# Order of all work as one table, and the units left over from both quads in one buffer

## The chip, the cores and the metric

The kernel runs on one core of a Trainium2 chip. The metric is the device time of one execution in microseconds; a median of several runs is given. TensorE (PE, with its weight loads as PEld), VectorE (DVE), ScalarE (ACT), GpSimd (POOL) and SyncE (SP, which here issues all DMAs) have a queue of instructions each and work it off in order.

## The reference, cut to what matters

Linear attention with exponential features, for 8 batches, 8 heads, 576 positions, heads of 64 and 128 features, and then a gated feed-forward layer with a convolution of width 3 along the positions:

```python
def phi(x):                                   # x: q or k
    proj = einsum('bhsd,df->bhsf', x, w_phi)
    proj = proj - max(abs(proj), axis=-1, keepdims=True)
    return concatenate([exp(proj), exp(-proj)], axis=-1)
kv  = einsum('bhsf,bhsd->bhfd', phi(k), v)
num = einsum('bhsf,bhfd->bhsd', phi(q), kv)
den = einsum('bhsf,bhf->bhs', phi(q), sum(phi(k), axis=2)) + 1e-06
x   = num / den                               # heads side by side: 512 columns
h   = maximum(x @ w_in, 0.0)                  # 512 -> 1024
c   = conv_w[0] * h[t-1] + conv_w[1] * h[t] + conv_w[2] * h[t+1]
out = (h * sigmoid(c)) @ w_out                # 1024 -> 512
```

The weights of the second part come as 64-bit floats, whose words the kernel turns into 32-bit values itself; its products run in three passes of split (high and low) values.

## The kernel before, in words

The heads of a batch form two quads of four, a quad is two head pairs. A unit is a piece of a quad's positions: units 1 and 2 hold 256 positions each, unit 0 holds the 64 positions that are left over, from both quads together. So a batch has five units of k and five of q, written (quad, unit).

A unit begins in `project`: two DMAs into the buffers "raw" (RAW of them), projections in 64\*64 tiles of TensorE into one PSUM bank for each head of a pair (the code's index i, then j), then for each of the two banks a maximum of absolute values on VectorE (L485) and a subtraction on VectorE (L492). In the first batch's k units a bank can be "biased" (KBU, 'b'): then there is no subtraction, ACT negates the maximum (L488) and takes exponentials of 128 columns straight from the bank, with the maximum as bias (L522).

`k_unit` loads v (two DMAs; V buffers), takes the exponentials (L518 or L522) and accumulates kv in 128\*64 tiles (L534 for unit 0, L549 else). After unit 2 ACT copies kv out (L557). `q_unit` transposes the features (L578, 128\*128 tiles), takes their exponentials (L582), multiplies by kv (L593, 128\*64 tiles), and divides: the denominator on ACT (L601) for the batches in DNA, on VectorE otherwise (L604), a reciprocal (L606) and a scaling into x (L607). In unit 0 each of the two banks has 256 columns, and each has its own transposes, exponentials, products and division.

Positions of all batches are then cut into 11 chunks of 320 to 448 (EDGES). `x_part` transposes x (L645) and splits it, `h_part` multiplies by w_in in eight groups h of 12 matmuls (L675), takes the positive part (L685), convolves (L688 on ACT, L698 on VectorE), takes the sigmoid and the gate (L704 to L719); `o_part` multiplies by w_out in four groups o of 24 matmuls (L739), copies out on ACT (L744) and stores. Weights are loaded and converted in `load_weight` during the first batches, mostly on VectorE and POOL with two works on ACT for each (L391, L400).

PSUM has four banks "g", two banks "m" (for h and o; x_part, the transposes and the numerators of q may use g and m, the first batch's k projections too) and two for kv.

What sets the order: the functions don't issue instructions, they add work items to a `Plan`, numbered in the order in which they are added, with a rank, a cost in nanoseconds, and the buffers that they read, write or take. `Plan.order` then plays the items through on a model of the five engines: at each step it takes the engine whose next item could begin first, and among the items that could begin then the one of the lowest rank. The table NUDGE shifts the rank of every group of items, and SLACK adds to the time at which an item of another engine releases one of TensorE. `place` picks the buffer that comes free first. The items are emitted in the order found, so each engine's queue has a fixed order in the compiled program.

Of the kernel before, what the change touches and what calls it, by code (L numbers as in the profile page):

```python
# [7 lines left out]
F32 = mybir.dt.float32  # L8
# [27 lines left out]
LANDING = 1600  # L36
PSUM_G = 4
# [12 lines left out]
SLACK = 60.0  # L50
# [9 lines left out]
RAW = 5  # L60
QS = 2
QE = 3
V = 2
OS = 2
KVF = 6
KBU = ('bb', 'bb', 'bb', 'bb', 'bb')
DNA = (0, 1)
# [3 lines left out]
NUDGE = """  # L71
# [43 lines left out]
"""  # L115
EDGE = [64 * n for n in EDGES]
# [27 lines left out]
class Plan:  # L144
# [7 lines left out]
    def add(self, eng, cost, hold, emit, reads=(), writes=(), rank=0.0, takes=(), tiled=0, table=None, after=(),  # L152
# [5 lines left out]
        w.ready = 0.0  # L158
# [75 lines left out]

    def order(self):
        engines = ("SP", "PE", "DVE", "ACT", "POOL")
# [4 lines left out]
        shift = [0.25 * int(x) for x in NUDGE.split()]  # L241
        if len(shift) == len(self.groups):
            for w in self.works:
                w.rank += shift[w.group]
# [5 lines left out]
        while len(out) < count:  # L250
# [50 lines left out]
            for o in w.before:  # L301
                o.ready = max(o.ready, w.end + HANDOVER[e, o.eng] + (SLACK if o.eng == "PE" and e != "PE" else 0))
                o.left -= 1
                if o.left == 0:
                    open_[o.eng].append(o)
# [4 lines left out]
def kernel(  # L310
# [33 lines left out]
    def dma(outp, inp, kb, rank, reads=(), writes=(), takes=()):  # L344
        cost = {130: 650, 128: 550, 64: 300, 512: 1600}.get(kb, 100 + 2 * kb)
        plan.add("SP", cost, 450, lambda: nc.sync.dma_start(out=outp(), in_=inp()), reads, writes, rank, takes)
# [108 lines left out]
    def project(src, b, qd, h, kind, r):  # L455
# [5 lines left out]
        for u in range(2):  # L461
            q, c0 = (u, 512) if h == 0 else (qd, u * 640 + (h - 1) * 256)
            dma(lambda u=u: raw[u](), lambda q=q, c0=c0: src[b, q, :, c0 : c0 + w], w // 2, r - 3.0, writes=w_(raw[u]))
        ps = [psum([P, 2 * n * F], f"p{nm}_{i}", M + G if b == 0 and kind == "k" else G) for i in range(2)]
        m = [piece([P, 2, 2 * n], F32, f"m{nm}_{i}", "m", 6) for i in range(2)]
        pr = [None if biased[i] else piece([P, 2 * n, F], F32, f"s{nm}_{i}", kind + "s", KS if kind == "k" else QS)
              for i in range(2)]

# [9 lines left out]
        for u in range(2):  # L478
            mm(222 * n, lambda u=u: emit(u), w_(raw[u], wbd_f), [(ps[0], u), (ps[1], u)], r + 0.01 * u,
               takes=[x for x in (*m, *pr) if x is not None], tiled=2)  # L480
        for i, p in enumerate(ps):
# [5 lines left out]
            if biased[i]:  # L487
                act(207, 95, lambda i=i: nc.scalar.activation(out=m[i]()[:, 1], in_=m[i]()[:, 0], func=AF.Copy, scale=-1.0),  # L488
                    [(m[i], 0)], [(m[i], 1)], ri)
            else:  # L490
                vec(*((681, 597) if n == 2 else (417, 331)),
                    lambda i=i, view=view: nc.vector.tensor_tensor(  # L492
                        out=pr[i](), in0=view(), in1=m[i]()[:, 0].unsqueeze(2).broadcast_to([P, 2 * n, F]),
                        op=ALU.subtract), w_(p) + [(m[i], 0)], w_(pr[i]), ri - 0.1)
# [4 lines left out]
    def k_unit(b, qd, h, r):  # L499
# [9 lines left out]
        es = []  # L509
        for j, p in enumerate(ps):  # L510
            rj = r + n // 2 * j
# [13 lines left out]
        if h == 0:  # L525
            for q in range(2):
# [12 lines left out]
                mm(880, emit, w_(*es[0], *es[1], vs[q]), w_(*kvps[b, q]), r + 1.0 + 4.0 * q, tiled=1)  # L539
# [23 lines left out]
    def q_unit(b, qd, h, r):  # L563
        n, ps, m, pr = project(qT, b, qd, h, "q", r)
        x = piece([P, n, 2, D], F32, f"x{b}_{qd}_{h}", "x0" if h == 0 else "x", 2 if h == 0 else NXX)
        for q in range(2):
            if h == 0 or q == qd:
                xs[b, q, h] = x
        for j in range(2):
# [275 lines left out]
```

## Time and profile before

| what | us |
|---|---|
| median of 3 runs | 708.52 |
| lowest, highest | 708.51, 711.76 |
| the profiled execution's own time | 710.4 |
| its span, first to last instruction | 708.4 |
| TensorE busy | 693.5 |
| TensorE weight loads busy | 639.3 |
| VectorE busy | 478.5 |
| ACT busy | 430.9 |
| POOL busy | 72.6 |

The profile is of one execution. A busy time is the union of an engine's instructions; a matmul's end is modelled, so successive matmuls overlap in it. "Idle before" is the time that the engine stood still just before a group, with what released it. The mean granted clock of TensorE over the span was 0.995.

### The profile page before, as it was taken

The page shows a single profiled execution, that of the slowest core. Times are in us where ns is not written, and L with a number is a line of the kernel's source. Part 1 is how long each engine was busy: PE and PEld are TensorE (multiplying, and loading weights), DVE is VectorE, ACT ScalarE, POOL GpSimd, SP SyncE. Part 2 cuts the span into 40 slices and gives each one's busy share as a digit, 9 for nine tenths or more (in the row PEclk, how much of TensorE's full clock was granted, in tenths as well). Part 3 has the DMA queues.
Part 4 walks back from the last instruction along what each step waited for, and adds up shares of the span by engine and source line. Part 5 has one row for each costly group of instructions (what it writes and reads, how often), then busy time and mean ns, then how long its engine had stood idle before and what let it go on. Part 6 is the DMA issues. An engine that isn't in the chain of part 4 may idle for free. (4 is left out here: it accounts for less than half of the span.)

```text
span 708.4 us, 22055 instructions
## 1 busy us (share of the span) xinstructions
PE 693.5 (98%) x9484; PEld 639.3 (90%) x9484; DVE 478.5 (68%) x1030; ACT 430.9 (61%) x821; POOL 72.6 (10%) x103
## 2 busy tenths in 40 slices
PE   6998999999999999999999999999999999999998
PEld 5886899899999999999999989999998899999997
DVE  4797998989796286776538675788259544567350
ACT  7977788785774465674349365755567343655351
POOL 0343213350010010000001000100100000101000
PEclk9999999999999999999999999999999999999999
DMA  7563543341212022222202311112002110000001
GB/s 211 163 203 112 153 116 101 103 110 50 69 58 61 22 71 79 73 70 66 64 13 76 106 42 46 57 33 61 27 27 70 35 40 15 14 24 13 36 27 52
DMA packets 46609, 49.00 MB, mean 69 GB/s; under 512 B 6320, under 2 KB 44464, under 8 KB 46512
## 3 DMA queue, kind: packets, MB, share of 16 engines
q1 hardware_dynamic: 46512, 47.59, 22.6%
q8 instruction: 75, 1.23, 0.7%
q14 instruction: 22, 0.18, 0.1%
HBM read 38.13 MB, written 9.44 MB: 67 GB/s over the span
## 5 line engine op out<-in xcount | busy, mean ns | idle before, releaser
L698 DVE SCALAR_TENSOR_TENSOR c<-h,cw,c 128x254 f32<-128x254 f32 (+11 forms) x256 | 122.7, 520 | 100.0 <-ACT c L688 98.7
L675 PE MATMUL hp<-xh,win_hi 128*128 128x448 f32 (+2 forms) x352 | 128.7, 366 | 0.8 <-ACT h L685 0.7
L739 PE MATMUL op<-gh,wout_hi 128*128 128x448 f32 (+3 forms) x352 | 127.6, 362 | 0.0
L739 PE MATMUL op<-gl,wout_hi 128*128 128x448 f32 (+3 forms) x352 | 124.7, 354 | 0.1
L739 PE MATMUL op<-gh,wout_lo 128*128 128x448 f32 (+3 forms) x352 | 124.3, 353 | 0.0
L675 PE MATMUL hp<-xh,win_lo 128*128 128x448 f32 (+2 forms) x352 | 123.9, 352 | 0.0
L675 PE MATMUL hp<-xl,win_hi 128*128 128x448 f32 (+2 forms) x352 | 123.8, 352 | 0.0
L582 ACT ACTIVATE qe<-tp 128x512 f32<-128x512 f32 (+1 forms) x160 | 79.8, 566 | 46.3 <-PE tp L578 46.0
L518 ACT ACTIVATE ke<-sk 128x512 f32<-128x512 f32 (+1 forms) x140 | 74.2, 595 | 41.2 <-DVE sk L492 22.0
L685 ACT ACTIVATE h<-hp 128x448 f32<-128x448 f32 (+2 forms) x88 | 45.5, 518 | 65.0 <-PE hp L675 63.7
L593 PE MATMUL nm<-kvf,qe 128*64 128x65 f32 x2304 | 78.9, 224 | 0.3 <-ACT qe L582 0.2
L682 POOL COPY h<-h 128x3 f32<-128x3 f32 x64 | 28.0, 437 | 478.3 <-DVE c L707 262.5
L593 PEld LDWEIGHTS nm<-kvf,qe 128*64 128x64 f32 x2304 | 73.3, 139 | 3.9 <-issue 2.7
L549 PE MATMUL kv<-v,ke 128*64 128x65 f32 x2048 | 72.5, 226 | 4.5 <-DMA v<-in_vt_dram 3.0
L549 PEld LDWEIGHTS kv<-v,ke 128*64 128x64 f32 x2048 | 66.5, 140 | 8.7 <-ACT w_t L391 3.3
L675 PEld LDWEIGHTS hp<-xh,win_hi 128*128 128x128 f32 x352 | 66.1, 188 | 7.1 <-issue 1.5
L739 PEld LDWEIGHTS op<-gh,wout_hi 128*128 128x128 f32 x352 | 66.2, 188 | 4.7 <-issue 1.2
L739 PEld LDWEIGHTS op<-gl,wout_hi 128*128 128x128 f32 x352 | 66.3, 188 | 4.0 <-DVE gl L719 0.3
L739 PEld LDWEIGHTS op<-gh,wout_lo 128*128 128x128 f32 x352 | 66.4, 189 | 3.3
L675 PEld LDWEIGHTS hp<-xl,win_hi 128*128 128x128 f32 x352 | 66.0, 188 | 3.5
L675 PEld LDWEIGHTS hp<-xh,win_lo 128*128 128x128 f32 x352 | 66.2, 188 | 3.1
L719 DVE TENSOR_TENSOR gl<-c,gh 128x896 fp32r<-128x896 f32 (+3 forms) x44 | 43.5, 1025 | 34.1 <-ACT gh L716 34.0
(58 smaller groups left out, 965.2 us busy)
## 6 DMA issues: line engine op xcount, KB each, us to landing
v<-in_vt_dram SPq DMA_DIRECT2D x80, 130.0 KB, 2.5
rk<-in_kT_dram SPq DMA_DIRECT2D x64, 128.0 KB, 2.6
rq<-in_qT_dram SPq DMA_DIRECT2D x64, 128.0 KB, 2.3
w_r<-in_w_in_dram SPq DMA_DIRECT2D x8, 512.0 KB, 4.1
w_r<-in_w_out_dram SPq DMA_DIRECT2D x8, 512.0 KB, 3.7
out_dram<-os SPq DMA_DIRECT2D x12, 191.0 KB, 2.0
out_dram<-os SPq DMA_DIRECT2D x12, 161.0 KB, 1.8
out_dram<-os SPq DMA_DIRECT2D x8, 225.0 KB, 2.3
```

The lines of the kernel that those rows point to most:

```text
L518: act(*((627, 520) if n == 4 else (417, 306)), lambda s=s, e=e, j=j: nc.scalar.activation(out=e[s](), in_=pr[j](), func=AF.Exp, scale=1.0 ...
L549: nc.tensor.matmul(out=kp()[a : a + 64, s, t // 2 * VW : (t // 2 + 1) * VW], lhsT=es[j][s]()[:, t, a : a + 64], rhs=vs[t // 2]()[:, c : c ...
L582: act(*((597, 478) if n == 4 else (384, 264)), lambda s=s, tp=tp, qe=qe: nc.scalar.activation(out=qe()[:, s], in_=tp(), func=AF.Exp, scale ...
L593: nc.tensor.matmul(out=ps_()[a : a + 64, t, :], lhsT=qe()[:, s, t, a : a + 64], rhs=kv[b, q][j]()[:, s, p0 * VW : (p0 + 1) * VW], start=(s ...
L675: nc.tensor.matmul(out=ps()[:, :W], lhsT=w, rhs=x, start=(p == 0 and k == 0), stop=(p == 3 and k == 2))
L682: pool(405, 375, lambda hs=hs, old=old: nc.gpsimd.tensor_copy(out=hs()[:, :3], in_=old[0]()[:, w0 - old[1] : w0 - old[1] + 3]), [(old[0], ...
L685: act(*cols(49, 0.84, W, 121), lambda ps=ps, hs=hs: nc.scalar.activation(out=hs()[:, 3 : 3 + W], in_=ps()[:, :W], func=AF.Relu), w_(ps), [ ...
L698: lambda f=f, hs=hs, j=j, lo=lo, hi=hi: nc.vector.scalar_tensor_tensor(out=c4()[:, f, lo - t0 : hi - t0], in0=hs()[:, at(lo) + j - 1 : at( ...
L719: vec(*cols(67, 1.04, 2 * N, 87), lambda f=f, a=a, gh4=gh4, gl4=gl4: nc.vector.tensor_tensor(out=gl4()[:, a : a + 2, :N], in0=c4()[:, f : ...
L739: nc.tensor.matmul(out=ps()[:, :N], lhsT=w, rhs=x, start=(i == 0), stop=(i == 23))
```

## The change

The order is no longer found by the planner: a table ORDER lists the numbers of all work items in the order in which they are emitted. If its length is the number of items, `order` returns `listed(keys)`, which goes through the table and gives each buffer the slot that is free and was used longest ago; no costs are read. NUDGE and SLACK go, and some costs and LANDING are other numbers.

With MG = 1, unit 0 holds both banks' features in one buffer: the subtractions write it interleaved, k's exponentials are two of 512 columns where there were four of 256, q's four transposes go into one PSUM bank, and there are two exponentials of 512 columns, one group of products, one denominator, one reciprocal and one scaling where there were two of each with half the columns. MP, NB and FD are 0 and change nothing.

Sizes: RAW 5 to 6, V 2 to 4, DNA from batches 0, 1 to batches 0 to 3. KBU: the first batch's k unit 0 has no biased bank any more, its other k units one in place of two.

```diff
-LANDING = 1600
-PSUM_G = 4
+LANDING = 1700
-SLACK = 60.0
-RAW = 5
+RAW = 6
-V = 2
+V = 4
-KBU = ('bb', 'bb', 'bb', 'bb', 'bb')
-DNA = (0, 1)
+KBU = ('uu', 'bu', 'bu', 'bu', 'bu')
+DNA = (0, 1, 2, 3)
-NUDGE = """
...
+ORDER = """
+0 3 4 5 6 178 7 179 180 181 192 8 193 194 195 182 184 183 9 185 189 196 214 188 197 215 205 198 186 203 202 201 217
+204 199 208 207 216 206 209 220 200 211 28 190 29 210 218 212 239 223 33 2 238 30 219 213 222 241 18 240 261 224 230
...
+3118 3119 3120 3127 3128 3129 3130 3131 3132
+PSUM_G = 4
+MP = 0
+NB = 0
+MG = 1
+FD = 0
...
+    def listed(self, keys):
+
+        out, last = [], {}
+        for i, key in enumerate(keys):
+            w = self.works[key]
+            for p in w.pieces:
+                if p.slot is None:
+                    free = [s for s in p.slots if s not in self.holder or self.holder[s].left == 0]
+                    p.slot = min(free, key=lambda s: last.get(s, -1))
+                    self.holder[p.slot] = p
+                p.left -= 1
+                last[p.slot] = i
+            assert all(d.end for d in w.after)
+            w.end = 1.0
+            out.append(w)
+        return out
+
     def order(self):
+        keys = [int(x) for x in ORDER.split()]
+        if len(keys) == len(self.works):
+            return self.listed(keys)
...
+        if MG and h == 0:
+
+            both = piece([P, 2 * n, 2, F], F32, f"s{nm}", kind + "s", KS if kind == "k" else QS)
+            pr = [None if biased[i] else both for i in range(2)]
...
-                        out=pr[i](), in0=view(), in1=m[i]()[:, 0].unsqueeze(2).broadcast_to([P, 2 * n, F]),
-                        op=ALU.subtract), w_(p) + [(m[i], 0)], w_(pr[i]), ri - 0.1)
+                        out=pr[i]()[:, :, i] if MG and h == 0 else pr[i](), in0=view(), in1=m[i]()[:, 0].unsqueeze(2).broadcast_to([P, 2 * n, F]),
+                        op=ALU.subtract), w_(p) + [(m[i], 0)], [(pr[i], i if MG and h == 0 else None)], ri - 0.1)
...
+        if MG and h == 0:
+            ee = [piece([P, 2, 2, F], F32, f"ke{b}_{qd}_{h}_{s}", "ke0", 2) for s in range(2)]
+            plan.group = f"{name}e"
+            for s in (1, 0):
+                if pr[0] is not None and pr[1] is not None:
+                    act(627, 520, lambda s=s: nc.scalar.activation(out=ee[s](), in_=pr[0](), func=AF.Exp, scale=1.0 - 2.0 * s),
+                        w_(pr[0]), w_(ee[s]), r, table="Exp")
+                    continue
...
+        if MG and h == 0:
+            plan.group = f"t{b}_{qd}_{h}_0"
+            tp = psum([P, 4, P], f"tp{b}_0", GM)
+            qe = piece([P, 2, 4, P], F32, f"qe{b}_0", "qe", QE)
+
+            def emit_tp():
+                for i in range(4):
+                    nc.tensor.transpose(out=tp()[:, i, :], in_=pr[0]()[:, i // 2, i % 2], identity=idn())
+
+            mm(109 * 4, emit_tp, w_(pr[0], idn), w_(tp), r, takes=(qe,), soft=50)
+            for s in (1, 0):
+                act(597, 478, lambda s=s: nc.scalar.activation(out=qe()[:, s], in_=tp(), func=AF.Exp, scale=1.0 - 2.0 * s),
+                    w_(tp), [(qe, s)], r, table="Exp")
+            ps_ = psum([P, 4, VW], f"nm{b}_0", GM + ["n_0"] * (NB > 0))
...
+            mm(234 * 4, emit, [(qe, 0), (qe, 1)] + w_(*kv[b, 0], *kv[b, 1]), w_(ps_), r, takes=(dn, rc, x), tiled=1)
...
+            vec(424, 332, lambda: nc.vector.tensor_tensor(
+                out=x().rearrange("p t j d -> p (t j) d"), in0=ps_()[:, :, :D],
+                in1=rc().unsqueeze(2).broadcast_to([P, 4, D]), op=ALU.mult), w_(ps_, rc), [(x, 0), (x, 1)], r - 0.3)
+            return
```

## Rows read from the trace of the kernel before

**Rows 1.** The page: busy time, share of the span and instructions of each engine.
```profile
PE 693.5 (98%) x9484; PEld 639.3 (90%) x9484; DVE 478.5 (68%) x1030; ACT 430.9 (61%) x821; POOL 72.6 (10%) x103
```
**Rows 2.** Windows: length; busy PE, PEld, DVE, ACT, POOL; clock; DMA share; GB/s.
```profile
0.00:20.00 20.00, 13.96 (x268) 12.26 (x268) 9.62 (x20) 15.73 (x57) 2.61 (x8) 0.96 0.69 206
20.00:40.00 20.00, 19.17 (x482) 17.13 (x480) 15.97 (x32) 19.16 (x61) 5.67 (x5) 0.95 0.62 185
40.00:60.00 20.00, 17.78 (x428) 15.96 (x422) 17.57 (x37) 15.75 (x36) 8.53 (x7) 0.91 0.53 155
60.00:80.00 20.00, 18.50 (x332) 15.16 (x330) 17.10 (x40) 14.82 (x35) 5.23 (x4) 1.00 0.42 123
80.00:100.00 20.00, 20.00 (x476) 18.32 (x474) 19.77 (x38) 15.09 (x33) 5.50 (x4) 1.00 0.49 145
100.00:130.00 30.00, 29.23 (x492) 26.51 (x487) 26.35 (x55) 25.17 (x50) 8.73 (x6) 1.00 0.36 104
130.00:700.00 570.00, 569.80 (x7010) 529.23 (x7009) 372.11 (x814) 324.31 (x554) 36.30 (x71) 1.00 0.17 51
```
**Rows 3.** Waits of TensorE: waiter, releaser: us in total, times, longest.
```profile
PE kv L549 <- DMA v<-in_vt_dram: 3.0, 2, 2.7
PE xt L645 <- DVE x L607: 1.9, 1, 1.9
PE pk L474 <- DMA rk<-in_kT_dram: 1.4, 1, 1.4
...
PE hp L675 <- ACT h L685: 0.7, 1, 0.7
```
**Rows 4.** Timeline of TensorE: start, length, line, operation, tiles, form, count.
```profile
31.79 1.10 PE L593 MATMUL nm<-kvf,qe 128*64 128x65 f32 x32
32.82 1.10 PE L474 MATMUL pk<-wbd_f,rk 64*64 64x128 f32 x32
33.86 1.09 PE L578 MATMUL tp<-idn,sq 128*128 128x128 f32 x8
...
88.19 0.34 PE L675 MATMUL hp<-xh,win_hi 128*128 128x384 f32 x1
88.36 0.34 PE L675 MATMUL hp<-xh,win_lo 128*128 128x384 f32 x1
...
95.79 1.10 PE L474 MATMUL pq<-wbd_f,rq 64*64 64x128 f32 x32
96.71 1.05 PE L474 MATMUL pk<-wbd_f,rk 64*64 64x128 f32 x32
...
98.68 1.10 PE L593 MATMUL nm<-kvf,qe 128*64 128x65 f32 x32
99.61 1.10 PE L549 MATMUL kv<-v,ke 128*64 128x65 f32 x32
```
**Rows 5.** Timeline of ACT: exponentials early, and the last copy.
```profile
6.22 2.69 ACT L522 ACTIVATE ke<-pk,mk 128x128 f32<-128x128 f32 x10
...
28.15 2.25 ACT L582 ACTIVATE qe<-tp 128x512 f32<-128x512 f32 x4
...
705.11 0.44 ACT L744 ACTIVATE os<-op 128x322 f32<-128x322 f32 x1 [3.10 <-PE op L739]
```
**Rows 6.** Groups by form, ACT: busy us, mean ns, idle before.
```profile
L582 ACT ACTIVATE qe<-tp 128x512 f32<-128x512 f32 x128 | 69.6, 612 | 40.6 <-PE tp L578 40.3
...
L582 ACT ACTIVATE qe<-tp 128x256 f32<-128x256 f32 x32 | 10.3, 384 | 5.7 <-PE tp L578 5.7
```
**Rows 7.** Timeline of VectorE, pieces of the first 92 us.
```profile
5.01 0.76 DVE L485 TENSOR_REDUCE mk<-pk 128x2 f32<-128x256 f32 x2 [5.01 <-PE pk L474]
...
84.40 1.28 DVE L485 TENSOR_REDUCE mk<-pk 128x4 f32<-128x512 f32 x2
85.59 1.27 DVE L492 TENSOR_TENSOR sk<-pk,mk 128x512 f32<-128x512 f32 x2
...
89.18 0.41 DVE L388 TENSOR_SCALAR w_t<-w_r 128x512 int32<-128x512 int32 x1
```

More of the change, by code (lines that the diff above doesn't have):

```diff
@@ L157, in add @@
         w.before = []
-        w.ready = 0.0
+        w.ready = w.end = 0.0
         w.group = self.groups.setdefault((self.group, eng), len(self.groups))
@@ L240, in order @@
         table, tiled, pipe, port = "Exp", 0, 0.0, {"DVE": 0.0, "POOL": 0.0}
[L241 to L244, printed above, removed]
         out = []
@@ L301, in order @@
             for o in w.before:
-                o.ready = max(o.ready, w.end + HANDOVER[e, o.eng] + (SLACK if o.eng == "PE" and e != "PE" else 0))
+                o.ready = max(o.ready, w.end + HANDOVER[e, o.eng])
                 o.left -= 1
@@ L344, in dma @@
     def dma(outp, inp, kb, rank, reads=(), writes=(), takes=()):
-        cost = {130: 650, 128: 550, 64: 300, 512: 1600}.get(kb, 100 + 2 * kb)
-        plan.add("SP", cost, 450, lambda: nc.sync.dma_start(out=outp(), in_=inp()), reads, writes, rank, takes)
+        cost = ({130: 470, 128: 465, 64: 310, 512: 1550} if FD else {130: 680, 128: 620, 64: 350, 512: 1550}).get(kb, 100 + 2 * kb)
+        plan.add("SP", cost, 240 if FD and kb in (130, 128, 64) and reads == () else 475, lambda: nc.sync.dma_start(out=outp(), in_=inp()), reads, writes, rank, takes)
     def vec(cost, hold, emit, reads, writes, rank, takes=(), port=False):
@@ L463, in project @@
             dma(lambda u=u: raw[u](), lambda q=q, c0=c0: src[b, q, :, c0 : c0 + w], w // 2, r - 3.0, writes=w_(raw[u]))
-        ps = [psum([P, 2 * n * F], f"p{nm}_{i}", M + G if b == 0 and kind == "k" else G) for i in range(2)]
+        ps = [psum([P, 2 * n * F], f"p{nm}_{i}", M + G if b == 0 and kind == "k" else GM if MP else G) for i in range(2)]
         m = [piece([P, 2, 2 * n], F32, f"m{nm}_{i}", "m", 6) for i in range(2)]
@@ L479, in project @@
             mm(222 * n, lambda u=u: emit(u), w_(raw[u], wbd_f), [(ps[0], u), (ps[1], u)], r + 0.01 * u,
-               takes=[x for x in (*m, *pr) if x is not None], tiled=2)
+               takes=list(dict.fromkeys(x for x in (*m, *pr) if x is not None)), tiled=2)
         for i, p in enumerate(ps):
@@ L509, in k_unit, with __init__, __call__ @@
         es = []
+        if MG and h == 0:
[6 more added lines that the diff above has]
+                    continue
+                for j, p in enumerate(ps):
+                    for i in range(2):
+                        act(393, 250, lambda s=s, i=i, j=j, p=p: nc.scalar.activation(
+                            out=ee[s]()[:, i, j], in_=p()[:, i * F : (i + 1) * F], func=AF.Exp, scale=1.0 - 2.0 * s,
+                            bias=m[j]()[:, 1 - s, i : i + 1]), [(p, None), (m[j], 1 - s)], [(ee[s], (i, j))], r + j, table="Exp")
+            class Part:
+                def __init__(self, e, j):
+                    self.e, self.j = e, j
+                def __call__(self):
+                    return self.e()[:, :, self.j]
+            es = [[Part(ee[s], j) for s in range(2)] for j in range(2)]
+            kes = ee
         for j, p in enumerate(ps):
+            if es and h == 0 and MG:
+                break
             rj = r + n // 2 * j
@@ L538, in k_unit @@
                 plan.group = f"{name}m{q}"
-                mm(880, emit, w_(*es[0], *es[1], vs[q]), w_(*kvps[b, q]), r + 1.0 + 4.0 * q, tiled=1)
+                mm(880, emit, w_(*(kes if MG else [*es[0], *es[1]]), vs[q]), w_(*kvps[b, q]), r + 1.0 + 4.0 * q, tiled=1)
             return
@@ L568, in q_unit, with emit @@
                 xs[b, q, h] = x
+        if MG and h == 0:
[10 more added lines that the diff above has]
+            ps_ = psum([P, 4, VW], f"nm{b}_0", GM + ["n_0"] * (NB > 0))
+            dn = piece([P, 4], F32, f"dn{b}_0", "dn", 4)
+            rc = piece([P, 4], F32, f"rc{b}_0", "rc", 4)
+            def emit():
+                for i in range(4):
+                    for s in (1, 0):
+                        for a in (0, 64):
+                            nc.tensor.matmul(out=ps_()[a : a + 64, i, :], lhsT=qe()[:, s, i, a : a + 64],
+                                             rhs=kv[b, i // 2][i % 2]()[:, s, a // 64 * VW : (a // 64 + 1) * VW],
+                                             start=(s == 1), stop=(s == 0))
+            plan.group = f"n{b}_{qd}_{h}_0"
+            mm(234 * 4, emit, [(qe, 0), (qe, 1)] + w_(*kv[b, 0], *kv[b, 1]), w_(ps_), r, takes=(dn, rc, x), tiled=1)
+            if b in DNA:
+                act(207, 95, lambda: nc.scalar.activation(out=dn(), in_=ps_()[:, :, D], func=AF.Copy, bias=1e-6), w_(ps_),
+                    w_(dn), r - 0.3)
+            else:
+                vec(150, 66, lambda: nc.vector.tensor_scalar(out=dn(), in0=ps_()[:, :, D], scalar1=1e-6, scalar2=None,
+                                                             op0=ALU.add), w_(ps_), w_(dn), r - 0.3)
+            vec(172, 85, lambda: nc.vector.reciprocal(out=rc(), in_=dn()), w_(dn), w_(rc), r - 0.3)
+            vec(424, 332, lambda: nc.vector.tensor_tensor(
+                out=x().rearrange("p t j d -> p (t j) d"), in0=ps_()[:, :, :D],
+                in1=rc().unsqueeze(2).broadcast_to([P, 4, D]), op=ALU.mult), w_(ps_, rc), [(x, 0), (x, 1)], r - 0.3)
+            return
         for j in range(2):
@@ L583, in q_unit @@
                     out=qe()[:, s], in_=tp(), func=AF.Exp, scale=1.0 - 2.0 * s), w_(tp), [(qe, s)], rj, table="Exp")
-            ps_ = psum([P, n, VW], f"nm{nm}", GM)
+            ps_ = psum([P, n, VW], f"nm{nm}", GM + ["n_0"] * (NB > 0) + ["n_1"] * (NB > 1 and h == 0))
             dn = piece([P, n], F32, f"dn{nm}", "dn", 4)
@@ L687, in h_part @@
             if CA:
-                act(*cols(49, 0.84, N, 121), lambda f=f, hs=hs: nc.scalar.activation(
+                act(*cols(188, 0.83, N, 110), lambda f=f, hs=hs: nc.scalar.activation(
                     out=c4()[:, f, :N], in_=hs()[:, at(t0) : at(t1)], func=AF.Copy, scale=cwv()[:, f, 1:2]),
```

167 rows, old and new, of tables (NUDGE, ORDER) are left out of this document.

## The prediction

> **What bounds the kernel now.** I read the engine totals first: TensorE is busy for 693.5 of 708.4 us, every other engine for less than 70% [rows 1]. So time can come only from TensorE's gaps, its clock, or work taken off it, and the question is where the gaps lie. The windows tell [rows 2]. Between 130 and 700 us TensorE is busy for 569.80 of 570.00 us: nothing is left there. Up to 130 us it is idle for 6.04 + 0.83 + 2.22 + 1.50 + 0 + 0.77 = 11.4 us, of which 1.0 is the start. The other 10.4 are waits [rows 3]: for the landing of v and of rk, for x (written by VectorE), for ACT behind h. A wait costs more than its idle time, because the idle time begins only when the last matmul's modelled end is reached: back to back a product of 32 instructions takes 0.93 us, and its row says 1.10 [rows 4]. With some 13 waits at about 0.2 to 0.25 us I add 3.0. The clock: the granted share is 0.96, 0.95 and 0.91 in the first three windows, then 1.00 [rows 2]; that is stretches at the 1.2 GHz level behind waits, and (0.04 + 0.05 + 0.09) x 20 = 3.6 us. **What order and feeding could win back is thus 10.4 + 3.0 + 3.6 = 17.0 us, all in the first 130 us.** The end can't be shortened by order: one ACT copy at 705.11 and a DMA follow the last matmul [rows 5], and both stay.
>
> What keeps TensorE waiting there is the feeding pair. VectorE is busy for 19.77 of 20 us in 80 to 100 and for 80.0 of the first 100; ACT for 19.16 of 20 in 20 to 40 [rows 2].
>
> **The change part by part.**
>
> *TensorE's work stays.* Projections, transposes, products and chunk matmuls are the same in number and shape. The units left over from both quads issue their four transposes as one group of four instead of two of two, and 16 products as one group; no instruction goes.
>
> *Switches of array form.* Each passage between 128\*128, 128\*64 and 64\*64 tiles costs time. Products followed by products start 0.93 apart, products followed by projections 1.03; projections followed by projections 0.92, by transposes 1.04 [rows 4]: 0.10 and 0.12, I take 0.11. Before has 151 passages (changes of form between neighbours in the order of the matmuls' starts). For after I numbered the work items as the code adds them (3133, the count of the table's entries) and read TensorE's entries in the table's order: 159. So the table adds 8 x 0.11 = **+0.9 us**. Bounds: 0 if an added passage falls into a wait, 8 x 0.34 = 2.7 if each cost a whole matmul duration, the chunk matmuls of [rows 4].
> The Trainium skill (TensorEngine Tiling (Array Packing), Tiling Modes, Key Properties) says that a change of tiling mode drains TensorE, which speaks against this change: a full drain at every added passage would be the 2.7 just named, and the sum 1.8 us worse. The rows show a third of that.
>
> *Left-over units in one buffer.* Per batch, four exponentials of 256 columns become two of 512, for q and for k; at 384 and 612 ns [rows 6] that takes 4 x 0.384 - 2 x 0.612 = 0.3 us off ACT, twice a batch, and one reciprocal, one denominator and one scaling off VectorE. After 130 us it is worth nothing to the end, since TensorE hides both engines; in the first 100 us it is in the sums below. Its price: the first exponential now needs both subtractions, one of 0.36 us more [rows 7]. Behind it in ACT's queue stand other units' exponentials, whose products TensorE would take next; with several units in hand that covers it, except in the very first unit, where ACT has nothing else to do and TensorE waits the 0.36 longer (it is in ACT's start below).
>
> *First k units half unbiased.* 40 of 72 exponentials of 128 columns (0.27 each [rows 5]: 10.8 us of ACT) go, about 10 of 512 come (0.56 each); VectorE gets 6 subtractions, 4 x 0.60 + 2 x 0.36 = 3.1 us [rows 7]. ACT is the fuller one before 40 us, VectorE after: each is in the sums.
>
> *More v and raw buffers (V 4, RAW 6).* A v transfer no longer waits until a product has left its buffer. The 3.0 us of waiting for v [rows 3] go; what is late next is ACT, below.
>
> *Denominators of batches 2 and 3 on ACT; SLACK, NUDGE, LANDING and the DMA costs.* The former moves small work off VectorE, the fuller engine from 60 to 130 us; worth 0 to 0.5 us. The latter are read only by the planner, which a full table bypasses: 0.
>
> *The order.* Here is the gain, and I bound it by loads: TensorE can't start an item before its feeder has worked off its own queue.
> ACT, up to the last exponential that the second numerator of q unit (0, 1, 1) needs, has 74 entries: 22 of 512 columns at 0.56 = 12.3, 32 of 128 at 0.27 = 8.6 [rows 5], and, estimated from the 512-column works by their width, 10 of weights at 0.6 = 6.0, 4 copies of kv at 0.35, 6 small at 0.1: 28.9 us. It starts after VectorE's first four works, 5.0 + 4 x 0.36 = 6.4 [rows 7], so it is there at 35.3. TensorE's entries ahead of that numerator are 16 projections at 0.46, 4 at 0.23, 14 products at 0.93, 4 groups of transposes at about 0.44 (an estimate: eight of them take under 1.0 in [rows 4]), 2.6 of warm-up: 26.7, with 21 passages 29.0, begun at 1.0: 30.0. **TensorE must have lost 5.3 us by then.**
> VectorE, up to the second subtraction of q unit (2, 0, 1), has 196 entries: 104 of 512 columns at 0.60, 25 masks of weights at 0.42, 40 of 256 at 0.36, 6 for chunk 0 at 0.60, 21 small ones 3.3 together [rows 7]: 94.2, from 5.0 on: 99.2. TensorE's entries ahead are 42 projections at 0.46, 12 at 0.23, 48 products at 0.93, 19 groups of transposes at 0.44 and four at 0.33, 17 chunk groups of three matmuls 0.17 to 0.18 apart [rows 4], 2.6 of warm-up: 88.0, with 59 passages 94.5, begun at 1.0: 95.5. **3.7 lost, plus whatever VectorE idles after 5.0.**
> So the least loss is 5.3. The most I take from before: VectorE idled 20.0 us of its first 100, 15 beyond the start [rows 2], which gives 3.7 + 15 = 18.7. Nearest to the new state is the 80 to 100 window, idle 0.23, and ACT's 20 to 40, idle 0.84, as the table leaves both queues almost as long as TensorE's at every point I added up; but the first 20 us can't be that dense, since ACT feeds TensorE there. I let VectorE idle 5 and take 8.5 lost. For the clock, less idle time should leave one of the two stretches at 1.2 GHz: 1.8 (bounds 0 and 3.6).
>
> **Sum.** 17.0 - 8.5 - 1.8 - 0.9 = 5.8 us less: the span goes from 708.4 to 702.6. The profiled execution itself took 710.4, 2.0 over its span; the median of the runs shown is 708.5, 0.1 over that span. So I predict 702.7 for the median.
>
> **The rivals.**
> *VectorE idles as before (slower).* The table fixes each engine's order, and an entry that waits holds all behind it: VectorE's works on weights stand between maxima that TensorE needs, and wait for ACT's two works on the same words. If it still idles 15 us by (2, 0, 1), TensorE loses 18.7 and 3.6 by the clock: 17.0 - 22.3 - 0.9 = 6.2 us more, 714.7. For it: ACT's busy share was 0.75 from 40 to 100 [rows 2], so the engines did wait for one another. Against: the v buffers and ACT's lighter first units remove two reasons. It decides from 11 us of idle time beyond the start on, where the change is worth nothing.
> *Two banks run short later (slower).* h and o groups share two PSUM banks, and the table interleaves them in ones and twos. Before has a single such wait, 0.7 us, hp from h [rows 3]. Nine new ones undo 6 us; twenty give 708.5 - 5.8 + 14 = 717. Against: 0.2 us idle in 570 before, with the same two banks [rows 2].
> *A wash.* The v wait goes, but ACT and VectorE end the next waits later: some 13 us lost of 17.0, clock 3.0, passages 0.9, so 708.4.
> *Packed tighter than I take.* Loss at the bound 5.3, full clock: 17.0 - 5.3 - 0.9 = 10.8 less, 697.7.
>
> **How the numbers follow.** Forecast and its neighbourhood (700 to 705) 0.47, tighter (below 700) 0.18, wash 0.20, idle VectorE 0.09, banks 0.06. Range 697.5 to 711: it leaves out half of each slower case and a little below. The likeliest alone: 700 to 705. A measurement tells 0.5%, 3.5 us, from no change: faster 0.64, same 0.20, slower 0.16.
>
> **What would show it.** Right: TensorE's idle time before 130 us near 6, no wait for v, clock 1.00 after about 25 us, VectorE idle under 7 us from 20 to 100, 130 to 690 as full as now. Wrong: idle time spread over the later windows, waits of hp and op for ACT, or VectorE's busy time by 100 us no higher than 80.

## The result and the profile after

The kernel after takes 698.42 us (median of 4, 697.9 to 699.55), the kernel before 709.04 (median of 4, 708.51 to 711.76): a ratio of 0.9845, 95% interval 0.9816 to 0.9873. It is 10.6 us faster by the medians, and 10.7 by the spans of the profiled executions (708.4 and 697.7, granted clock 1.000 after). The profile after is of the slowest of the four executions, whose spans are 696.1 to 697.7.

The page after, to be held against [rows 1]:

```profile
span 697.7 us, 21888 instructions
PE 689.1 (99%) x9484; PEld 635.7 (91%) x9484; DVE 476.4 (68%) x996; ACT 421.4 (60%) x771; POOL 64.4 (9%) x103
```

TensorE has the same 9484 matmuls, and is busy 4.4 us less for them. Its idle time, span less busy, went from 14.9 to 8.6 us. The windows after, columns as in [rows 2], say where:

```profile
0.00:20.00 20.00, 17.03 (x351) 14.36 (x353) 11.98 (x23) 14.03 (x41) 1.84 (x7) 1.00 0.68 203
20.00:40.00 20.00, 18.74 (x474) 16.26 (x470) 19.73 (x40) 17.07 (x43) 7.79 (x6) 1.00 0.71 210
40.00:60.00 20.00, 19.02 (x532) 17.30 (x532) 18.76 (x43) 17.32 (x40) 6.40 (x5) 1.00 0.56 157
60.00:80.00 20.00, 20.00 (x436) 17.85 (x432) 18.91 (x44) 15.69 (x35) 7.57 (x7) 1.00 0.59 191
80.00:100.00 20.00, 20.00 (x435) 18.40 (x431) 19.37 (x43) 16.55 (x37) 5.82 (x5) 1.00 0.46 130
100.00:130.00 30.00, 29.99 (x546) 27.88 (x546) 28.12 (x55) 24.88 (x48) 5.77 (x7) 1.00 0.39 110
130.00:690.00 560.00, 560.00 (x6702) 519.60 (x6701) 359.51 (x755) 314.98 (x532) 29.17 (x68) 1.00 0.17 49
```

Up to 130 us TensorE is idle for 2.97 + 1.26 + 0.98 + 0 + 0 + 0.01 = 5.2 us, 1.0 of it the start; before it was 11.4. The clock is 1.00 in all windows, which gives back the 3.6 us that it cost before. VectorE is nearly full from 20 us on, where before it got there after 80. So 10.7 = 6.2 of idle time + 3.6 of clock + 0.9 of busy time that is left (refills saved less passages added). How much TensorE idles early on differs between executions of the same orders: up to 60 us it is 5.2 us here, and 2.7 and 3.5 in runs 3 and 4 below, which change nothing before 60 us. Nothing after 130 us has a part in it, and the end is the same: one copy, as in [rows 5], 3.3 us before the end of either span.

```profile
694.39 0.44 ACT L914 ACTIVATE os<-op 128x322 f32<-128x322 f32 x1 [3.10 <-PE op L909]
```

TensorE's waits after, form as in [rows 3]:

```profile
PE spare L479 <- POOL bias_e L472: 1.0, 1, 1.0
PE xt L815 <- DVE x L777: 1.0, 1, 1.0
PE nm L763 <- issue: 0.9, 1, 0.9
PE pk L581 <- DMA rk<-in_kT_dram: 0.8, 3, 0.3
PE kv L681 <- ACT ke L654: 0.7, 1, 0.7
PE kv L681 <- ACT ke L650: 0.6, 1, 0.6
```

The wait for v, 3.0 us, is gone; none is above 1.0. The early ACT queue shows half-biased units, eight short exponentials followed by two long ones, where [rows 5] has ten short ones in a row. First column the start, second the length:

```profile
8.51 2.16 ACT L654 ACTIVATE ke<-pk,mk 128x128 f32<-128x128 f32 x8
10.51 1.20 ACT L650 ACTIVATE ke<-sk 128x512 f32<-128x512 f32 x2
```

And the groups by form have lost the 256-column exponentials of [rows 6]:

```profile
L752 ACT ACTIVATE qe<-tp 128x512 f32<-128x512 f32 x128 | 72.0, 604 | 23.5 <-PE tp L748 23.4
```

### The profile page after: what moved, and what is told of

The parts are those of the page before. It is cut to its first block, busy times and chain, and to the rows that moved or that the text cites. A ratio compares the mean times of both kernels' runs of the same rounds, so it can differ in the third digit from the quotient of the medians.

```text
span 697.7 us, 21888 instructions
## 1 busy us (share of the span) xinstructions
PE 689.1 (99%) x9484; PEld 635.7 (91%) x9484; DVE 476.4 (68%) x996; ACT 421.4 (60%) x771; POOL 64.4 (9%) x103
## 4 chain that ended last, share of the span: by engine, by line
PE 94%; ACT 2%; DMA 2%; DVE 1%; issue 1%; SPq 0%; ACTq 0%; DVEq 0%
PE hp L845 29%; PE op L909 29%; PE nm L763 9%; PE kv L681 8%; PE pq L581 5%; PE pk L581 5%; PE tp L748 4%; PE xt L815 3%; PE kv L666 2%; PE nm L722 1%; DMA rk<-in_kT_dram 1%; DMA w_r<-in_w_in_dram 1%; ACT ke L654 1%; ACT ke L650 1%; PE tp L708 0%
## 5 line engine op out<-in xcount | busy, mean ns | idle before, releaser
L868 DVE SCALAR_TENSOR_TENSOR c<-h,cw,c 128x321 f32<-128x321 f32 (+11 forms) x256 | 119.0, 515 | 65.0 <-ACT c L858 64.5
L752 ACT ACTIVATE qe<-tp 128x512 f32<-128x512 f32 x128 | 72.0, 604 | 23.5 <-PE tp L748 23.4
L650 ACT ACTIVATE ke<-sk 128x512 f32<-128x512 f32 x120 | 71.8, 639 | 16.0 <-DVE sk L599 13.3
L592 DVE TENSOR_REDUCE mq<-pq 128x4 f32<-128x512 f32 (+1 forms) x80 | 49.3, 629 | 33.6 <-PE pq L581 33.5
L681 PE MATMUL kv<-v,ke 128*64 128x65 f32 x2048 | 68.9, 223 | 1.5 <-ACT ke L654 0.7
L763 PE MATMUL nm<-kvf,qe 128*64 128x65 f32 x2048 | 68.7, 223 | 1.0 <-issue 0.9
L763 PEld LDWEIGHTS nm<-kvf,qe 128*64 128x64 f32 x2048 | 63.8, 138 | 5.7 <-issue 4.6
L681 PEld LDWEIGHTS kv<-v,ke 128*64 128x64 f32 x2048 | 64.2, 138 | 5.1 <-issue 2.7
L852 POOL COPY h<-h 128x3 f32<-128x3 f32 x64 | 20.8, 325 | 487.4 <-DVE c L877 256.0
```

The source lines that it names most:

```text
L592: lambda i=i, view=view: nc.vector.tensor_reduce(out=m[i]()[:, 0], in_=view(), axis=AX, op=ALU.max, apply_absolute_value=True), w_(p), [(m ...
L650: act(*((627, 520) if n == 4 else (417, 306)), lambda s=s, e=e, j=j: nc.scalar.activation(out=e[s](), in_=pr[j](), func=AF.Exp, scale=1.0 ...
L681: nc.tensor.matmul(out=kp()[a : a + 64, s, t // 2 * VW : (t // 2 + 1) * VW], lhsT=es[j][s]()[:, t, a : a + 64], rhs=vs[t // 2]()[:, c : c ...
L752: act(*((597, 478) if n == 4 else (384, 264)), lambda s=s, tp=tp, qe=qe: nc.scalar.activation(out=qe()[:, s], in_=tp(), func=AF.Exp, scale ...
L763: nc.tensor.matmul(out=ps_()[a : a + 64, t, :], lhsT=qe()[:, s, t, a : a + 64], rhs=kv[b, q][j]()[:, s, p0 * VW : (p0 + 1) * VW], start=(s ...
L868: lambda f=f, hs=hs, j=j, lo=lo, hi=hi: nc.vector.scalar_tensor_tensor(out=c4()[:, f, lo - t0 : hi - t0], in0=hs()[:, at(lo) + j - 1 : at( ...
```

## The experiments

**1. All first k units biased again, in the same table.** The negations and short exponentials stand where the subtractions and long ones stood; the orders of TensorE, SP and POOL are those of the kernel after.

```diff
-KBU = ('uu', 'bu', 'bu', 'bu', 'bu')
+KBU = ('bb', 'bb', 'bb', 'bb', 'bb')
```

> The changed kernel and its table, but the first batch's k units biased in both banks as before (KBU all 'bb'): ACT gets 40 exponentials of 128 columns at 0.27 us (10.8) and 6 negations (0.6) for 10 of 512 columns at 0.56 (5.6), so 5.8 us more work in its first 27 us; VectorE loses 6 subtractions, 3.1 us. Theory A (ACT's queue sets TensorE's loss in the first 35 us, VectorE's queue has cover): 4 to 6 us more, 702.4 to 704.4, and up to 1.8 more if the clock falls again. Rival V (VectorE's queue up to 100 us sets the loss, as its load sum in the prediction said): no slower, 696 to 698.4.

Measured: 708.51 us (10 runs), ratio to before 0.9992 [0.9977, 1.0008]; the whole gain is undone. Two windows and the waits:

```profile
0.00:20.00 20.00, 16.60 (x276) 13.53 (x280) 7.86 (x15) 15.73 (x58) 0.51 (x7) 0.94 0.66 193
20.00:40.00 20.00, 17.27 (x425) 15.00 (x419) 14.84 (x31) 18.18 (x54) 7.82 (x6) 0.97 0.63 192
```
```profile
PE kv L681 <- ACT ke L654: 2.2, 3, 1.1
PE hp L845 <- ACT qe L752: 1.7, 1, 1.7
PE pq L581 <- DVE sk L599: 1.4, 2, 1.2
PE pq L581 <- DVE x L777: 1.2, 1, 1.2
PE pk L581 <- ACT qe L752: 1.0, 1, 1.0
...
PE pq L581 <- ACT ke L654: 0.8, 1, 0.8
PE nm L763 <- DVE sk L599: 0.7, 1, 0.7
PE pk L581 <- DVE sq L599: 0.3, 1, 0.3
```

The rival, VectorE as what sets the early loss, predicted 696 to 698.4 and falls. My own theory gave at most 704.4 (706.2 with the clock): the loss is larger than the ACT work put back (5.9 us, 427.3 busy against 421.4), and it doesn't end at 40 us: TensorE still loses 1.62 us from 60 to 80 and 1.58 from 80 to 100, where it lost nothing.

The waits say why, and the run isn't the clean exchange that it was meant to be. Only kv from ke, 2.2 us, waits for a result of ACT's longer queue. In the others a projection, a product or an h group waits until something else has finished with a buffer, mostly a PSUM bank. `listed` gives each piece the free slot that was used longest ago, and with other work on the banks it deals them anew: by the two kernels' code, 460 of the 513 PSUM pieces lie in another bank than in the kernel after. The h group that waits 1.7 us for qe now has a bank whose last reader stands one entry ahead of it in the list; in the kernel after, the last reader of its bank stands six entries ahead. The waits of pq for x (1.2) and for sk (1.4), and of nm for sk (0.7), come about in the same way: one or two entries where the kernel after has four or more. Together these are 5.0 us, nearly all of the 5.6 us that TensorE idles more up to 130 us than in the kernel after. Without them and their five refills run 1 would take some 702.4 us, an estimate from these rows, and within what my theory had. So the run doesn't show that the half-biased units are worth 10 us; what they are worth with the banks held fixed isn't measured.

**2. Six needless 256-column exponentials on ACT**, spread over 15 to 50 us (extra work, 2.1 us in all; every other queue as in the kernel after).

```diff
+    for _ in range(6):
+        act(420, 330, lambda: nc.scalar.activation(out=dump(), in_=wbd_f(), func=AF.Exp), w_(wbd_f), w_(dump), 0.0, table="Exp")
```

> The changed kernel with six needless exponentials of 256 columns (some 0.36 us each, 2.1 in all) put into ACT's queue between 15 and 50 us. Theory A (ACT sets the loss there): 1.5 to 2.2 us more, 700 to 700.6. Rival V (VectorE sets it, ACT has cover): 698.4, within 0.5.

Measured: 699.48 us, ratio 0.9847 [0.983, 0.9865]. That is 1.1 us above the kernel after by the medians and nothing by the two ratios to before, whose intervals reach 1.3 us and more to either side: between the two forecasts. The trace decides more. TensorE's idle time up to 130 us is 5.3 us, as in the kernel after (5.2), and behind the first added exponential, at 17.1 us, its only wait for ACT is one of 0.2. So the load added to ACT's queue was mostly covered, and the price of 1.5 to 2.2 us isn't borne out; that it was nothing at all the times don't show.

**3. Six needless 256-column additions on VectorE**, spread over 60 to 95 us (extra work; the same edit with `vec` and `nc.vector.tensor_tensor`).

> The changed kernel with six needless additions of 256 columns (0.36 us each, 2.1 in all) in VectorE's queue between 60 and 95 us, where VectorE is 95% to 97% busy and TensorE never idle. Theory A: cover holds, 698.4 within 0.5. Rival V (VectorE's queue up to 105 us is what the end hangs on): 1.5 to 2.2 us more, 700 to 700.6.

Measured: 699.5 us, ratio 0.9851 [0.983, 0.9872], span 697.6. Again this is 1.1 us above the kernel after by the medians, less by the ratios, and between the two forecasts. VectorE is busy 19.81 of 20 us from 60 to 80, at no cost there. But at 91 to 93 us TensorE stands still twice, 1.1 us together, where it never does in the kernel after:

```profile
80.00:100.00 20.00, 18.93 (x422) 16.80 (x425) 19.29 (x43) 15.51 (x35) 5.55 (x5) 1.00 0.42 120
```
```profile
PE pk L580 <- DVE rc L775: 0.8, 1, 0.8
PE pk L580 <- issue: 0.3, 1, 0.3
```

The span is still no longer, because TensorE idled 2.5 us less in the first 60 us, ahead of the first addition at 63.6. It came to these waits that much earlier, which may be a part of their reason. So VectorE's cover is thin there: up to 1.1 of the 2.1 us was paid, neither nothing nor the whole.

**4. More passages.** Thirteen of TensorE's 962 entries, twelve quarters of h or o groups and one group of transposes, moved a few places ahead into runs of other tiles: 185 passages between array forms in place of 159, the other queues in their order. One of them, by the names of the entries:

```diff
+h2_2 p0
 q3_1_2 proj0
...
-h2_2 p0
 h2_2 p1
```

> The changed kernel with 13 chunk groups of the stretch from 150 us on moved between the projections of two units: 185 passages between array forms for 159, all other queues in the same order. At the 0.11 us of the prediction 26 passages cost 2.9 us: 701.3. If each drained TensorE for a whole matmul duration (0.34): 8.8 us, 707.2. If a passage costs nothing: 698.4.

Measured: 709.1 us (10 runs), span 707.2, 9.5 more than the kernel after. Not all of it is passages:

```profile
PE tp L747 <- DVE sq L598: 2.7, 1, 2.7
...
PE tp L747 <- DVE rc L775: 0.7, 1, 0.7
```
```profile
190.00:200.00 10.00, 7.30 (x98) 6.02 (x97) 3.82 (x7) 6.88 (x12) 0.93 (x5) 0.91 0.32 93
200.00:220.00 20.00, 20.00 (x309) 17.79 (x308) 13.39 (x25) 10.38 (x21) 0.19 (x1) 0.96 0.19 55
```

TensorE is idle 10.9 us in all (707.2 less a busy time of 696.3), 2.3 more than after: the moved transposes now stand ahead of their subtraction (2.7 us), a fault of the experiment; the clock falls behind the 2.7 us wait, which costs 0.9 + 0.8 = 1.7; and 266 of the 513 PSUM pieces lie in other banks. TensorE's busy time grew by 7.2; without the clock that leaves 5.5 for 26 passages and the refills of four new waits (0.9). That is 0.18 to 0.21 each, nearly twice my 0.11, and below 0.34. The busy time of the kernel after, run 2 and run 3, with the same work of TensorE, is 688.6 to 690.4, so anything from 0.13 to 0.23 fits. The Trainium skill (TensorEngine Tiling (Array Packing), Tiling Modes, Key Properties) says that a change of tiling mode drains TensorE. This run agrees that a change costs time, some 0.4 to 0.7 of a chunk matmul's 0.34 us.

**5. V 4 and RAW 6 alone, banks in turn.** The kernel before, its own order on every engine, fed through the new routine that gives every piece the slot that was used longest ago.

```diff
-RAW = 5
+RAW = 6
-V = 2
+V = 4
```

> The kernel before with its own order of instructions on every engine, with only the buffers changed: V 4 and RAW 6 (v and raw DMAs can start earlier). Theory (ACT's queue is what TensorE meets next): the 3.0 us of waiting for v go and come back in part as waits for ACT's exponentials within the next 20 us; the time falls by 0 to 2.5 us, 706 to 708.5. Rival (v buffers carry the gain): 3.0 of idle time, 0.7 of refills and a stretch of low clock, 1.8, go: 703 or less.

Measured: 716.44 us, ratio 1.0091 [1.0068, 1.0114]: outside both. With the engines' orders unchanged and only slots different, TensorE stood half of 60 to 70 us:

```profile
60.00:65.00 5.00, 2.39 (x19) 1.55 (x19) 0.97 (x3) 1.62 (x3) 0.00 (x0) 0.70 0.02 7
65.00:70.00 5.00, 2.63 (x29) 2.20 (x31) 2.31 (x6) 0.00 (x0) 1.39 (x1) 0.50 0.46 131
```
```profile
PE hp L778 <- DVE xl L754: 2.9, 1, 2.9
PE hp L778 <- ACT qe L685: 2.9, 1, 2.9
PE kv L652 <- DMA v<-in_vt_dram: 2.7, 1, 2.7
```

An h group waits for the bank out of which ACT takes exponentials: which bank a piece gets was part of the old order. The clock fell to 0.70 and 0.50 there, too. v is waited for as before; as the run mixes two edits, its time says nothing of v, and run 9 separates them.

**6 and 7. The planner in place of the table**, once with all the sizes of the kernel after, once the kernel before without its nudges.

```diff
-ORDER = """ ... """
+ORDER = ""
```
```diff
-NUDGE = """ ... """
+NUDGE = ""
```

> The kernel after without its table and without nudges: the planner finds the order; units left over together, half-unbiased first k units, V 4, RAW 6 and DNA stay. Theory (the sizes make room, and the table packs it: both are needed): TensorE idle well above the 5.2 us of the kernel after up to 130 us, some 8 to 14, 703 to 709. Rival (the lighter ACT load alone carries the gain): 697.5 to 700.5.

> The kernel before without its nudges: what its planner finds by costs and ranks alone, the counterpart of the kernel after without its table. Theory: the nudges were worth several us up to 130 us: 710 to 718, and above the kernel after without its table by 3 us or more, which is the share of the sizes under one and the same planner. Rival (sizes are worth nothing without the table): the two planned kernels within 1.5 us of each other.

Measured: 719.64 us, ratio 1.0143 [1.0128, 1.0158], and 728.43, ratio 1.0268 [1.025, 1.0287]. Planned without nudges, the kernel after is 8.8 us below the kernel before; that is the share of the merged units, half-biased banks, V, RAW and DNA together with the changed costs and LANDING and the missing SLACK, all of which the planner reads. The nudges were worth 19 us in the kernel before, the table 21 in the kernel after. The rival of run 7, within 1.5 us, falls. Both forecasts of run 6 and the theory's 710 to 718 for run 7 were too low.

**8. Left-over units taken apart again**, the table mapped as near as the buffers allow.

```diff
-MG = 1
+MG = 0
```

> The kernel after with the left-over units taken apart again (MG 0: two transposes' banks, exponentials of 256 columns, two products groups, two divisions), the table mapped on to the same order as near as the buffers allow. Theory (the merging is hidden by TensorE but for 0.3 us of ACT per unit, and for the first units' cover of 2 us): 698.4 to 700. Rival (the merged units carry a real part, as they spare ACT and VectorE work in the first 100 us): 702 or more.

Measured: 745.0 us, ratio 1.0512 [1.0482, 1.0541]. By the number the rival is right, but the run doesn't price the merging. The separate pieces need more of the same small pools, so the queues of TensorE, VectorE and ACT all differ from the table's, and waits stand everywhere up to 500 us (an o group for x 5.1 us, projections for sq 3.9). What the merged units are worth by themselves stays open.

**9 and 10. The other corners of a square: order by bias.** Both have the order of the kernel before, V 4, RAW 6, and every bank and buffer but v and raw as the old planner chose it. Run 10 also has the half-biased units (its new works stand where the old ones stood; TensorE's queue differs at 8 places, for the two buffers of subtracted features). The edit of run 10 beside run 9:

```diff
-KBU = ('bb', 'bb', 'bb', 'bb', 'bb')
+KBU = ('uu', 'bu', 'bu', 'bu', 'bu')
```

> The kernel before, its own order on every engine, every PSUM bank and buffer as its planner chose it; only v (4 buffers) and raw (6) go round in turn. The earlier run with V 4 also let the banks go round in turn, and TensorE stood 5 us at 65 us for that. Theory (behind v stands ACT's queue): 3.0 us of waiting for v go, waits for ACT's exponentials take most of their place; 706 to 709. Rival (the wait for v was worth its idle time, its refills and a stretch of low clock): 703.5 or less.

> As the run with V 4 and fixed banks, and the first batch's k units half unbiased as in the kernel after; the new subtractions and exponentials stand in the old order where the negations and biased exponentials stood. With the kernel after, the table with all banks biased, and the old order with all biased this is the fourth corner of a square (order by bias, all with V 4). Theory (the two need each other: an order is laid out for the load that it was found for): 704 to 709. Rival (ACT's load alone sets the early loss, 5.2 us of ACT work taken off): 698 to 702.

Measured, as ratios to before:

| | all biased | half biased |
|---|---|---|
| old order, V 4 | 0.998 [0.996, 1.0] (run 9) | 0.9996 [0.9973, 1.0018] (run 10) |
| table, V 4 | 0.9992 [0.9977, 1.0008] (run 1) | 0.9845 [0.9816, 0.9873] (the kernel after) |

Three corners are the kernel before, within 0.2%, and the fourth is 1.5% faster. The rivals of both runs fall (703.5 or less, 698 to 702); run 9's 708.22 us is inside its theory's range, run 10's 710.57 just above its own.

But the square doesn't show that order and load need each other. Its lower row also has the merged units and DNA for four batches, and its left lower corner has the banks dealt anew, which by the estimate there makes more than half of that corner's loss (run 1). What stands is the upper row, where every bank is as before: more buffers and half-biased units bring nothing to the old order. There v is waited for in both, longer than before. Run 9's waits, and the same for run 10:

```profile
PE kv L788 <- DMA v<-in_vt_dram: 4.4, 2, 4.2
PE hp L914 <- ACT qe L821: 1.8, 1, 1.8
```
```profile
PE kv L781 <- DMA v<-in_vt_dram: 4.3, 1, 4.3
```

The DMA issues tell why the wait stays, from the timeline of SP's queue (start, length, what is loaded), first of run 9, then of the kernel after:

```profile
12.22 0.33 SPq L585 DMA_DIRECT2D rq<-in_qT_dram  x1
13.76 0.33 SPq L585 DMA_DIRECT2D rk<-in_kT_dram  x1
14.14 1.10 SPq L585 DMA_DIRECT2D v<-in_vt_dram  x2
17.77 0.33 SPq L585 DMA_DIRECT2D w_r<-in_w_in_dram  x1
```
```profile
10.84 0.80 SPq L449 DMA_DIRECT2D rq<-in_qT_dram  x2
11.70 2.19 SPq L449 DMA_DIRECT2D v<-in_vt_dram  x3
```

In run 9 v goes out right behind a transfer of k that itself had to wait, so a free buffer of v doesn't bring it forward; the kernel before issues the two at 13.96, no later. The products that need it start at 17.84, 1.5 us later than before: from issue to landing a v transfer takes 3.7 us by the median between 8 and 22 us, 2.4 before, for a reason that isn't shown. The table puts three v transfers ahead, at 11.70, and there is no such wait. Whether it could do so with two buffers, and whether half-biased units would pay in the old order with v moved forward, no run shows.

**11 and 12. Two other tables for the kernel after**, found by small moves in the old one against a replay of its traced durations: 157 and 154 passages, the same work. The first lines of run 12's table:

```diff
-0 3 4 5 6 178 7 179 180 181 192 8 193 194 195 182 184 183 9 185 189 196 214 188 197 215 205 198 186 203 202 201 217
...
+0 178 179 193 192 214 201 186 3 215 4 5 6 7 8 9 180 181 194 195 184 182 185 183 188 196 198 189 216 199 202 197 205
...
```

> The kernel after with another table, found by small moves in the old one on a replay of its traced durations: 157 passages instead of 159, the same work. Theory (what is left is 4.2 us of waits up to 130 us, 1 of refills, and 0.11 for each passage): 694 to 697. Rival (the moves trade waits that the replay sees for others that it does not, such as a late DMA or a bank): 698.5 or more.

> The same from another start of the search: 154 passages instead of 159. Theory: 693.5 to 697. Rival: 698.5 or more.

Measured: 701.55 us, ratio 0.9877 [0.9835, 0.9919], and 696.15 (695.31 to 698.13), ratio 0.9805 [0.9767, 0.9843]. The first is its rival's: waits that the replay didn't have, a late q transfer 1.7 us and 1.3 us of idle time after 130. The second has the lowest time of all, 2.3 us below the kernel after by the medians; the intervals of the two ratios overlap, so that it beats the kernel before is shown, that it beats the kernel after is likely. It fills 20 to 130 us further, and pays a wait of 2 us early on, with the clock behind it. (This is the slowest of its executions; in two of the others the mean clock is 1.000.)

```profile
0.00:20.00 20.00, 16.04 (x320) 14.46 (x324) 10.99 (x20) 13.85 (x39) 1.71 (x7) 0.92 0.78 228
20.00:40.00 20.00, 19.37 (x476) 16.82 (x468) 19.03 (x41) 18.15 (x45) 6.93 (x6) 0.99 0.56 162
40.00:60.00 20.00, 20.00 (x560) 18.07 (x560) 19.75 (x45) 17.27 (x38) 6.46 (x6) 1.00 0.65 183
```
```profile
PE kv L680 <- ACT ke L653: 2.0, 1, 2.0
```

## Why the prediction was right, and where it was not

*What bounds it, and where the gain is.* Right: all of it came from the first 130 us, and the ceiling of 17.0 us held (10.7 were won).

*The size, 5.8 against 10.7.* The step that failed is "I let VectorE idle 5 and take 8.5 lost. For the clock [...] 1.8". By the waits, 4.2 us of idle time and about 1.6 of refills (seven waits at the prediction's 0.23, for which its rows show 0.17) were lost, 5.8 in place of 8.5, and the clock took 0 in place of 1.8. Those two are 4.5 of the 4.9 us between forecast and result. The case that came true is "packed tighter", 697.7, but partly by luck: its loss of 5.3 was a bound on ACT that didn't hold (below).

*Why 8.5 was too much.* I added VectorE's own idle time to a 3.7 us lead of its load over TensorE's. VectorE did idle 6.2 us up to 100 us beyond its start at 5.03, more than the 5 I let it. But TensorE's sum, 95.5, was some 4 us short: after, the second transposes of q unit (2, 0, 1) begin at 105.50, with 5.2 us of idle time and 1.6 of refills ahead of them, which makes the work about 98.7 against my 94.5. So the lead wasn't there. VectorE's subtraction (the second of these lines) ends at 105.02, half a us before the transposes that take it, and TensorE works on chunks meanwhile:

```profile
103.02 0.68 DVE L599 TENSOR_TENSOR sq<-pq,mq 128x512 f32<-128x512 f32 x1
...
104.33 0.69 DVE L599 TENSOR_TENSOR sq<-pq,mq 128x512 f32<-128x512 f32 x1
```
```profile
105.33 0.34 PE L845 MATMUL hp<-xl,win_hi 128*128 128x384 f32 x1
105.50 0.60 PE L748 MATMUL tp<-idn,sq 128*128 128x128 f32 x4
```

*What the sum left out.* 18 chunk groups stand ahead of these transposes in the table, not 17, which is 0.5 us. The rest is the size of what I gave a passage: with run 4's 0.18 to 0.21 us in place of 0.11, the 59 passages ahead add 4.1 to 5.9 us, an estimate as rough as that price, but as large as the gap. By it one term set too low, the passage, made VectorE look 3.7 us later than TensorE.

*ACT's bound, 5.3 lost by the second numerator of (0, 1, 1).* Right about ACT, wrong about TensorE. I had ACT there at 35.3, and the last exponential for it ended at 34.73, with the numerator 0.1 behind it:

```profile
34.12 0.61 ACT L752 ACTIVATE qe<-tp 128x512 f32<-128x512 f32 x1
```
```profile
34.82 0.41 PE L763 MATMUL nm<-kvf,qe 128*64 128x65 f32 x8
```

But TensorE's terms add up to 25.7, not to the 26.7 of the prediction, so by my own working it had to lose 6.3 by then. It had idled 2.3 us beyond the start, with about 1.1 of refills: 3.4 lost. Its own work took 30.4 us in place of 28.0; at run 4's price the 21 passages make 1.5 to 2.1 of that difference, and the rest is open. Nor is the bound a price for each entry, since run 2 put 2.1 us more into 15 to 50 us of that queue and TensorE's idle time stayed at 5.3.

*The v buffers, "a v transfer no longer waits until a product has left its buffer. The 3.0 us [...] go".* Wrong as a cause. More buffers alone leave a v wait of 4.4 us (run 9); it is gone where the table also sets v further ahead in SP's queue.

*The half-biased units, costed at their load.* Open. Taken back in the table, with the banks dealt anew, they cost 10 us, of which more than half is the banks by the estimate there (run 1); put into the old order, where v is late, they bring nothing (run 10). The prediction had no term for where pieces lie, and run 1 and run 5 show that it can be the largest. Which part of the change carries how much of the 10.7 us is therefore not shown. That the gain lies in the waits and the clock up to 130 us is shown.

*Passages, +0.9.* Undersized: run 4 gives about 0.2 each, 1.6 for the eight, and more for the sums above. *Left-over units:* not tested cleanly. *DNA, 0 to 0.5:* not tested.

*The rivals.* No h or o group waits for a bank in the kernel after; that rival appeared instead where banks were dealt anew (runs 1 and 5). VectorE's idle time, 6.2 us, stayed below the 11 from which it was to decide. The signs named all came: idle time 5.2 (near 6), no v wait, clock 1.00 (in the first window too), VectorE's idle time from 20 to 100 us 3.2 (below 7), 130 to 690 full.

## What to carry to other kernels

An order written out is also a choice of banks and buffers. To price one part of such a change, exchange it alone and hold the slots as well as the orders; then see in the waits whether something is waited for as a result or as a place. A bound by the sum of one queue's load is only as good as the same sum for the engine that waits on it; check it at a point that the old trace already shows. Another buffer for v didn't help while a transfer that waited stood ahead of v in SP's queue (run 9).

## What the runs showed of the hardware

In these runs the clock fell to the 1.2 GHz level behind waits, but a wait's length alone doesn't say when: it fell behind a wait of 1.09 us at 17 us in run 1 (with one of 0.83 us six us earlier), behind 1.95 in run 12, 1.93 and 2.7 before. The h group at the same place in the order waited 1.79 us at 60 us in run 9 and the clock stayed; it waited 1.66 us at 61 us in run 10 and the clock fell. Each fall behind a wait of these lengths cost 1.7 us, by the shares in the windows that it lay in. No wait of the kernel after is above 1.0 us, and it kept 1.00 in every window.

Where pieces lie weighed more than a full queue. 2.1 us of work put into ACT's or VectorE's full stretch cost 1.1 us at most by the medians (runs 2 and 3). With the same orders on every engine and the same buffer counts, other banks and slots alone made 8 us (run 5 against run 9, 716.44 and 708.22 us, ratios 1.0091 and 0.998).
